# Second layer 7 steps behind instead of 8, Wo's last 64 columns as column-tiled head pairs, FFN up in 128-row chunks plus tails, and a new instruction order

## Chip, cores, metric

One core of one Trainium2 chip. The metric is device time in microseconds (us), the median of several executions. The kernel before takes 2892.89 us (median of 3 runs, 2892.76 to 2893.84).

## The reference

Two identical layers over x of 2048 x 576, bfloat16. Each adds a memory-augmented recurrent attention of the layer norm (32 heads of 128; 64 segments of 32 rows, each with 8 memory rows that the segment before produced), then a gated FFN (576 -> 4608 -> 576) of the layer norm.

```python
for s in range(n_seg):                       # 64 segments, strictly in order
    h = concat([mem, x[:, s*32:(s+1)*32]])   # 40 rows
    q, k, v = h @ Wq, h @ Wk, h @ Wv         # 32 heads x 128
    o = softmax(mask(q @ k.T * scale)) @ v
    o = einsum('bhte,hed->btd', o, Wo)
    mem = o[:, :8]; outs.append(o[:, 8:])
# FFN: (silu(x @ w1) * (x @ w3)) @ w2
```

## The kernel before

Both layers run interleaved: in step t, layer 0 works on segment t and layer 1 on segment t - LAG. So the first and the last LAG steps hold one layer (40 columns, N=40 per matmul) and the steps between two (N=80). FFN groups ("jobs") take 128 rows of one layer or of both (N=128 or 256); jobs 0, 1 and 16 have one layer and run in the first 16 steps and the last ones; job 17 comes after the attention. TensorE's order is a fixed string, one letter for a piece: Q/q are Q,K and their row tail, S scores, T transposes of the probabilities, P times V, O Wo, F/f FFN up and tail, W FFN down, V/v/X/x the values.

```python
LAG = 8
POOLS = {"bank": 7, "y": 1, ..., "ot": 1, ..., "w13": 2, "w2": 3, "htt": 4}
...
def layers_of(t):
    return [li for li in (0, 1) if 0 <= t - LAG * li < nseg]
...
ORDER = FIRST + FOUR * 11 + LAST            # one letter for each piece of TensorE
...
def wo(self, t, g, ot):                     # 8 heads x 5 column blocks
    for hl in range(GH):
        for db in range(5):
            d0 = min(db * P, D - P)         # the last block overlaps the fourth
            self.mm(yT[:, db, :], self.T.WO[:, GH * g + hl, d0:d0 + P], OT[:, hl, :], ...)
...
def ffn_up(self, ents, pr, w13, b, last, tail=None):
    for fb in range(2):
        ...
        for c in ((8,) if tail else range(NCH)):      # NCH = 9 chunks of 64 rows
            for r in (0, 1):                          # gate and up, side by side
                rr = slice(r * R64, (r + 1) * R64)
                self.mm(self.bk(b[r])[:, os_], W[rr, c, fs],
                        self.T.XTB[rr, 4 if tail else POS[c], lo:hi], ..., tile_position=(r * R64, 0))
...
def xtb_write(self, bi, b, split):          # the layer norm, transposed, to both halves
    for r in (0, R64):
        self.cp(n, dst[r:r + R64, 0:4, :], ps[0:R64, 0:4, :])
        self.cp(n, dst[r:r + R64, 4:NCH, :], ps[R64:P, 0:5, :])
```

Of the kernel before, what the change touches and what calls it, by code (L numbers as in the profile page):

```python
# [28 lines left out]
LAG = 8  # L29
# [6 lines left out]

POS = [c // 2 if c % 2 == 0 else 4 + c // 2 for c in range(NCH - 1)] + [8]
POOLS = {"bank": 7, "y": 1, "qkt": 4, "vx": 2, "vm": 1, "sme": 2, "pb0": 1, "pb1": 1, "pts": 1, "ot": 1,
# [10 lines left out]
class Node:  # L49
# [11 lines left out]
    def after(self, *more):  # L61
        for d in more:
# [7 lines left out]
         "WO": "O", "VX": "X", "VXt": "x", "VM": "V", "VMt": "v", "FF": "F", "FFt": "f", "W2": "W"}  # L70
# [108 lines left out]
def ewh(*ns):  # L179
# [5 lines left out]
    "maQQqqXVvxQSQXqQqSTqQPOTqPOSQxqTQqPSOTPXOxQQqqQqSQQqVSqvQTQqqQqPSTOSPOTPTOPaOQQqqQSqXQqQTSxQqqVvSQQqqPSTOPTOPTOP"  # L185
    "OQQqqQQSqVqQSvQqqQTQqPqSXTOSPTOPOTxPXOxQpQqqVSQQqqnvQQSqqFTQQSqPqFOSTFPWTOPFTOPFOXxQQqqQQSqFqQWQSqqFVvSTQQqPqWTO"
    "PSFOTFPTOWPFOaXxQQqqQQqSVqvQSqFQqWTQSPFqQqTOSPTOWPFTOPFOQQqqFVWQqSQvqFQQSqqFTQPqSWQOTqPSFTOPWTOPObVXxvQQqqpQSXqx"
    "QnqQQTSqqQPSFqOQTqFPSFOTPFXxOTWPFOVvQqQQqqFSQQqqXxSQqWTQSPqFOTQqFPSTOWPFXTOxPFOWaQQqqQQSqqQVqSXvxQQqFqWTSQPFTOqP"
    "FSOTFPXWTOxPFOFQQqQqQSqqQqXVvxQqSTSQPqWQOTqPFSOTWPFOTWPObppQXVqxnQqXxQqSQqnQqvQSqQTqFPFSTOQPqWOTSWPFOTXPFFxOWWQQ"
    "qqQSqVXxvQQqqQSqTQSPqFOTQqFPSWTOFPWTOFPFXxWWOQQqqWSVXxvQaTQqqQQSqFqQQSqqFPWTOFPTWOSWPFXTOWPxXOWQqFxQQqFqSQqVQvSQ"  # L190
    "qqQTWqSQWPqFTOPSTOPFOTWPWObVXxvpXxp"
)
FOUR = (
    "QQqqnQnQSqqQQSqqFTQqFPSQTOqPFSOWTWFPFTOXPxWOWQQqqFSQQqqXVxvSWQTQqqFPSQQTOqqFPWTOaSPFXxOTWPFOWQQqqVvSWQQqqFTQQSqq"
    "FPXSxOWTQQqqFFPSWTOWPFOTXxPFWOWQQqqVSvQQqqQQTSqqQQqPqSXxOTFPSWTOWPFTOWPWObVXxvppXx"
)
LAST = (
    "QQqqQSnQqqQQqqSnTQPFqFSTOQPqFSOTWWPFXTOPFOxQQqqXxQQSqqWQSWQqqFFVSvTQqPQqTOPSTOFPXOxTWPWOFQQqqWWQQqqFSSQQqqVXxvWT"
    "QqPSQTqOSFPWTOPFXTOxPWOWQQqFqQQqqFXSxQQSqqFTWQVvqQSqPWOTFPSFOTWWPFOTWPWObVvpQpQqqXxSQQqqnQnSqXxTQQqqQSqFPFTOSPTO"
    "FPFTOPWOWQQqqVWWvSQQqFqQSqQTqQQqqSPFTOXPSxTOWPFOTFPWOFQqQqFSWWQqQQqFqVvSWTWQqFPFTWOQSqPQOWqFTSFPXWFxTOWPFOWQQqqQ"  # L200
    "SQqqVSvQQqqTQSPqQqTOSPWOTFPTOWPOWpbVXvxnQQqqQQSqFqQQSqqXQTxSqQPqFTOSPWTOFPFTOPWOXxFQQqqQSqFVvQTqFSQWQqqFPSQQFqqO"
    "TWPSTOPFOTFPXOFxQWQqqQQSqqQqVSFvQTqQPqFSWQqTOSPFTOPFOTWPOQQqqQQSqVvqFQTqSQqPQSqQqWTSOPOTFPTOPOpnWFfFfFfFWFfFfWfF"
    "fFWfFFWffFfFfWFfFWFffFfWFfFfWW"
# [4 lines left out]
class Opt:  # L208

    qk, qkt, sc, tr, pv, wo, wog, vm = 0.0079, -0.0342, 0.0268, 0.1447, 0.0406, 0.2653, 0.0725, 0.1407  # L210
    vmt, vx, vxt, ff, fft, win, w2, gstep = -0.0231, 0.2313, 0.0843, 0.2124, -0.1839, 3.5294, 0.1943, 0.0624
    ustep, mode_pen, hor, wait, bulk, ff_split, last_win, tail_at = 0.0315, 0.1194, 0.0162, 0.141, 0.02, False, 3.0, -1.5


def make_nodes(em, nseg, pools, o=Opt, dma_bw=230e3, load_bw=340e3):
# [25 lines left out]
    for what, i in [("qk", 0), ("qk", 1), ("v", 0), ("v", 1), ("v", 2), ("v", 3), ("qk", 2), ("qk", 3), ("o", 0),  # L241
                    ("qk", 4), ("qk", 5), ("o", 1), ("qk", 6), ("qk", 7), ("o", 2), ("o", 3)]:
        pr += 0.1
        if what == "qk":
            ld_qk[i] = load("ldqk", kb(1152, 512), pr, em.load_qk(i))
        elif what == "v":
            ld_v[i] = load("ldv", kb(576, 1024), pr, em.load_v(i))
        else:
            ld_o[i] = load("ldo", kb(1024, 576), pr, em.load_o(i))
# [49 lines left out]
    def step(t):  # L299
# [22 lines left out]
        y = Slot("y", users=1)  # L322
        wos = []
        for g in range(NG):
            r, k = g // 2, g % 2
            qs, qe = [], []
            for u in (2 * g, 2 * g + 1):
# [8 lines left out]
                for kind in (0, 1):  # L336
# [22 lines left out]
            wo = node("PE", 40 * mm80, em.wo(t, g, ot), deps=ote + ([ld_o[g]] if t == 0 else []), prio=t + o.wo + o.wog * g, mode="full",  # L359
                      acq=[y] if g == 0 else [], rel=[ot], name="WO")  # L360
            if g:
                wo.after(wos[0])
            wos.append(wo)
            me[f"SC{g}"], me[f"TR{g}"], me[f"PV{g}"], me[f"WO{g}"] = sc, tr, pv, wo
        if t == nst - 1:
            last_reads[1].extend(me[f"QKt{u}"] for u in range(8))
            last_reads[2].extend(wos[:2])
        nxt = [li for li in ls if t - LAG * li + 1 < nseg]
        ye = []
        if nxt:  # L370
            m = 8 * len(nxt)
            ye.append(node("ACT", actc(4 * m), em.y_mem(t, nxt, 0), deps=wos, prio=t - 0.01, name="Ymem"))
            ye.append(node("ACT", actc(m, m), em.y_mem(t, nxt, 1), deps=wos, prio=t - 0.005, name="Ymem"))
            ye[1].after(ye[0])
        ht_mem[t + 1] += ye
        yts = node("ACT", actc(*([160] * nl)), em.yts(t, ls), deps=wos + ye, prio=t + 0.01, rel=[y], name="YTS")
# [3 lines left out]
    def post(li, g):  # L380

        b = banks(1)
        prio = 4 * g + 4 + LAG * li + 0.0
        d = node("PE", 5 * 0.056, em.post_tr(li, g, b[0]), deps=[yx[li, 4 * g + j] for j in range(4)] + ([xr_ld[g]] if li == 0 else []),
                 prio=prio, mode="full", acq=b, name="POST")
        return node("DVE", dve(576), em.post_add(li, g, xr[g], b[0]), deps=[d], prio=prio, rel=b, name="POSTa")
# [4 lines left out]
    def job(j):  # L391
# [6 lines left out]
        s0 = 4 * j + 4  # L398
# [4 lines left out]
        split = last or o.ff_split  # L403
        cost = ewh(512, 128, 128) if split else ewh(512, 640, 512, 640)
        for (bi, g) in ents:
            pa = post(bi, g)
            wr.append(ln_nodes("F", xr[g], Slot("xn"), [pa], s0, (lambda bi=bi: lambda b: em.xtb_write(bi, b, split))(), cost, [prev_ff]))
# [12 lines left out]
        for pp in range(NPR // 2):  # L420
            mids, w2s, htts, lds = [], [], [], []
            for pr_ in (2 * pp, 2 * pp + 1):
# [12 lines left out]
                if split:  # L435
                    fm = node("PE", 16 * mm, em.ffn_up(ents, pr_, w13, b, last, False), deps=wr + ld, prio=prio, mode="full",
                              acq=b + [htt], name="FF")
                    ff = node("PE", 2 * mm, em.ffn_up(ents, pr_, w13, b, last, True), deps=[fm], prio=prio + o.fft, mode="row",
                              rel=rel13, name="FFt")
                else:  # L440
                    ff = node("PE", 18 * mm, em.ffn_up(ents, pr_, w13, b, last), deps=wr + ld, prio=prio, mode="row",
                              acq=b + [htt], rel=rel13, name="FF")
# [12 lines left out]
        for (bi, g) in ents:  # L455
            if bi == 0:
                ht_ready[1, g] = ln_nodes("L1", xr[g], Slot("xn"), w2_last[0], s0 + 3.8,
                                          (lambda g=g: lambda b: em.ht_write(1, g, b))(), HTW, ht_wdeps(4 * g + LAG))
            else:
                xn = Slot("xn")  # L460
                c = node("ACT", actc(576), em.fin_cast(xr[g], xn), deps=w2_last[1], prio=s0 + 3.8, acq=[xn], rel=[xr[g]], name="fin")
                node("SWD", 1.0, em.store(g, xn), deps=[c], prio=s0 + 3.8, rel=[xn], lat=3.0, name="store")
# [17 lines left out]
    for t in range(nst):  # L480
# [7 lines left out]
        if t % 4 == 3:  # L488
            job((t + 1) // 4 - 1)
        if t + 1 < nst:  # L490
# [9 lines left out]
class Emitter:  # L500
# [93 lines left out]
    def load_w13(self, pr, w13):  # L594
        def f(n):
            fa = pr * 2 * P
            for r, wd in ((0, self.a.w1), (R64, self.a.w3)):
                self.dma(self.T.W13[r:r + R64, w13.i], wd[:, fa:fa + 2 * P].rearrange("(c p) f -> p c f", p=R64))
# [113 lines left out]
    def xtb_write(self, bi, b, split):  # L712
        def f(n):
            ps = self.lnps(b)
            dst = self.T.XTB[:, :, bi * P:(bi + 1) * P]
            if split:
                self.cp(n, dst[:, 0:4, :], ps[:, 0:4, :])
            for r in (0, R64):
                if split:
                    self.cp(n, dst[r:r + R64, 4, :], ps[R64:P, 4, :])  # L720
                else:
                    self.cp(n, dst[r:r + R64, 0:4, :], ps[0:R64, 0:4, :])
                    self.cp(n, dst[r:r + R64, 4:NCH, :], ps[R64:P, 0:5, :])
# [187 lines left out]
    def wo(self, t, g, ot):  # L911
        def f(n):
            yT, nq = self.yT(t)
            OT = self.T.OT[:, ot.i, 0:GH * nq].rearrange("p (h q) -> p h q", h=GH)
            for hl in range(GH):
                for db in range(5):
                    d0 = min(db * P, D - P)
                    self.mm(yT[:, db, :], self.T.WO[:, GH * g + hl, d0:d0 + P], OT[:, hl, :],
                            g == 0 and hl == 0 and db == 0, g == NG - 1 and hl == GH - 1 and db == 4)
        return f  # L920

    def y_mem(self, t, nxt, tail):
        def f(n):
# [7 lines left out]
            else:  # L931
                for r in (0, R64):
                    self.cp(n, H_[r:r + R64, 4, c0:c1], v[R64:P, 4])
        return f

    def yts(self, t, ls):
        def f(n):
            yT, _ = self.yT(t)
            j = t % 4
            for li in ls:  # L940
                c0 = XO[li] - ls[0] * QW
                self.cp(n, self.T.YTS[:, li, :, j * SEG:(j + 1) * SEG], yT[:, :, c0:c0 + SEG])
        return f

    def post_tr(self, li, g, b):
        def f(n):
            for db in range(5):
# [15 lines left out]
    def ffn_up(self, ents, pr, w13, b, last, tail=None):  # L963

        def f(n):
            lo, hi = self.span(ents)
            W = self.tail_w[pr][0] if last else self.T.W13[:, w13.i]
            for fb in range(2):
                fs = slice(fb * P, (fb + 1) * P)
                os_ = slice(fb * 2 * P + lo, fb * 2 * P + hi)  # L970
                if tail is False:
                    for r in (0, 1):
                        for c in range(4):
                            self.mm(self.bk(b[r])[:, os_], W[:, 4 * r + c, fs], self.T.XTB[:, c, lo:hi], fb == 0 and c == 0, False)
                    continue
                for c in ((8,) if tail else range(NCH)):
                    for r in (0, 1):
                        rr = slice(r * R64, (r + 1) * R64)
                        self.mm(self.bk(b[r])[:, os_], W[rr, c, fs], self.T.XTB[rr, 4 if tail else POS[c], lo:hi],
                                c == 0, c == NCH - 1, tile_position=(r * R64, 0))  # L980
# [173 lines left out]
```

## Time and profile before

| | value | how to read it |
|---|---|---|
| span | 2885.8 us | the profiled execution, first instruction to last |
| TensorE | 97% busy, x67733 matmuls | busy holds latency too |
| steady four steps | 166 us | eleven alike |
| waits on TensorE, by my sum | 138.8 us | trace minus slots and changes of mode, as in the prediction |

The timeline of TensorE gives start, length, matmuls; in brackets the idle time before.

```profile
2765.05 1.18 PE L519 MATMUL bank<-XTB,W 64*128 64x128 bf16 x36
2766.07 0.36 PE L519 MATMUL bank<-HT,W 64*128 64x40 bf16 x16
2766.36 0.77 PE L519 MATMUL YB<-OT,WO 128*128 128x40 bf16 x24
2769.32 0.57 PE L519 MATMUL YB<-OT,WO 128*128 128x40 bf16 x16 [2.19 <-issue]
```

A single Wo piece of 40 matmuls stops after its 24th for 2.4 us. All its operands were there: the first 24 read the same tiles. No semaphore and no buffer explains a stop in the middle of a piece.

### The profile page before, as it was taken

What the parts mean: (1) busy time and instruction counts of PE and PEld (TensorE: products, weight loads), DVE (VectorE), ACT (ScalarE), POOL (GpSimd) and SP (SyncE); (2) the same over time, 40 slices, a digit from 0 to 9 for tenths busy, and PEclk for the clock granted to TensorE, in tenths of its full rate; (3) what the DMA queues carried; (4) which work ended last, traced back from release to release, by engine and by line L of the source; (5) the groups of instructions that cost most, each with busy time, mean ns of one, the idle gap of its engine ahead of it and who ended that gap; (6) DMA issues with size and microseconds to landing.
All of it is one profiled execution on the core that took longest, in us unless ns stands there. A gap on an engine that the chain in (4) does not pass through costs nothing.

```text
span 2885.8 us, 147090 instructions
## 1 busy us (share of the span) xinstructions
PE 2801.2 (97%) x67733; PEld 2302.7 (80%) x67733; DVE 2077.1 (72%) x5053; ACT 1139.2 (39%) x2933; POOL 63.1 (2%) x110
## 2 busy tenths in 40 slices
PE   5999999999999999999999999999999999999987
PEld 4777878888888878888888888888888888888776
DVE  3667777776777778677777777677777767777765
ACT  1433443343444344344444434344433434343432
POOL 0000000000000000000000000000000000000000
PEclk8999999999999999999999999999999999999999
DMA  9055544434443444444344444534354343436467
GB/s 306 4 130 122 129 98 107 105 90 117 101 106 86 108 107 101 100 109 110 87 107 99 104 101 101 126 88 98 91 120 101 94 118 91 93 97 140 112 159 231
DMA packets 483563, 324.45 MB, mean 112 GB/s; under 512 B 16888, under 2 KB 478080, under 8 KB 482944
## 3 DMA queue, kind: packets, MB, share of 16 engines
q1 hardware_dynamic: 479872, 307.96, 44.3%
q8 instruction: 529, 8.67, 1.3%
q0 software_dynamic: 3072, 7.08, 0.8%
q14 instruction: 90, 0.74, 0.1%
HBM read 310.26 MB, written 2.36 MB: 108 GB/s over the span
## 4 chain that ended last, share of the span: by engine, by line
PE 83%; issue 6%; DVE 5%; DMA 4%; ACT 1%; SPq 1%; POOL 0%; POOLq 0%; DVEq 0%; ACTq 0%
PE bank L519 72%; PE YB L519 10%; DMA W<-in_B_w_dram 2%; DMA W<-in_A_Wk_dram 1%; DVE XR L525 1%; DVE HTT L525 1%; DVE STAT L525 1%; SPq L528 1%; DVE LNS L525 1%; DVE PB L525 1%; DVE SME L525 1%; DMA W2C<-in_B_w_dram 1%; DVE OT L525 0%; DVE XN L525 0%; ACT SME L522 0%
## 5 line engine op out<-in xcount | busy, mean ns | idle before, releaser
L519 PEld LDWEIGHTS <-W 128*128 128x128 bf16 (+1 forms) x34256 | 1231.1, 97 | 124.2 <-issue 34.3
L519 PE MATMUL bank<-HT,W 128*128 128x80 bf16 (+2 forms) x23040 | 805.9, 197 | 13.3 <-ACT HT L522 3.9
L519 PE MATMUL bank<-XTB,W 64*128 64x256 bf16 (+1 forms) x11216 | 616.6, 259 | 6.3 <-DMA W<-in_B_w_dram 4.6
L519 PE MATMUL bank<-WV,HT 128*32 128x512 bf16 (+3 forms) x8000 | 451.6, 384 | 11.3 <-DMA WV<-in_A_Wv_dram 10.1
L519 PE MATMUL YB<-OT,WO 128*128 128x80 bf16 (+1 forms) x11520 | 437.9, 198 | 14.2 <-issue 7.0
L522 ACT ACTIVATE QKT<-bank 128x320 bf16<-128x320 f32 (+1 forms) x773 | 272.9, 409 | 434.1 <-PE bank L519 430.8
L519 PEld LDWEIGHTS <-WO 128*128 128x128 bf16 x11560 | 412.3, 99 | 37.6 <-issue 31.3
L519 PEld LDWEIGHTS <-HT 128*32 128x32 bf16 (+3 forms) x8000 | 172.4, 93 | 219.0 <-issue 68.0
L525 DVE TENSOR_TENSOR PB<-SME,STAT 40x256 bf16<-40x256 f32 (+1 forms) x1024 | 320.5, 318 | 16.6
L519 PE MATMUL bank<-W2C,HTT 128*128 128x288 bf16 x2232 | 324.9, 288 | 5.6 <-DVE HTT L525 2.5
L525 DVE TENSOR_REDUCE STAT<-SME 104x8 f32<-104x320 f32 (+1 forms) x576 | 276.4, 480 | 67.7 <-ACT SME L522 59.9
L522 ACT ACTIVATE HTT<-bank 128x512 bf16<-128x512 f32 (+1 forms) x324 | 177.8, 549 | 341.7 <-PE bank L519 341.6
L525 DVE SCALAR_TENSOR_TENSOR HTT<-HTT,bank 128x512 bf16<-128x512 bf16 (+1 forms) x324 | 201.6, 622 | 107.8 <-ACT HTT L522 103.3
L525 DVE SCALAR_TENSOR_TENSOR XR<-bank,XR 128x288 f32<-128x288 f32 x576 | 245.1, 448 | 32.6 <-PE bank L519 27.8
L525 DVE CAST QKT<-bank 128x320 bf16<-128x320 f32 (+1 forms) x379 | 159.2, 443 | 137.8 <-PE bank L519 135.8
L519 PEld LDWEIGHTS <-HTT 128*128 128x128 bf16 x2304 | 205.0, 98 | 66.7 <-issue 10.5
L522 ACT ACTIVATE PTS<-bank 128x320 bf16<-128x320 f32 (+1 forms) x389 | 146.1, 404 | 197.8 <-PE bank L519 189.9
L525 DVE TENSOR_TENSOR HTT<-HTT,bank 128x512 bf16<-128x512 bf16 (+1 forms) x324 | 203.4, 628 | 23.3 <-DVE HTT L525 1.8
L522 ACT ACTIVATE SME<-SME 104x320 f32<-104x320 f32 (+1 forms) x288 | 135.0, 469 | 192.5 <-DVE SME L525 188.9
L525 DVE TENSOR_TENSOR SME<-bank,maskb 104x320 f32<-104x320 f32 (+1 forms) x288 | 140.1, 487 | 89.1 <-PE bank L519 84.5
L522 ACT ACTIVATE OT<-bank 128x320 bf16<-128x320 f32 (+1 forms) x346 | 133.2, 404 | 162.6 <-PE bank L519 155.9
L522 ACT ACTIVATE VX<-bank 128x512 bf16<-128x512 f32 x166 | 95.1, 596 | 179.7 <-PE bank L519 179.5
(65 smaller groups left out, 1878.4 us busy)
## 6 DMA issues: line engine op xcount, KB each, us to landing
W<-in_B_w_dram SPq DMA_DIRECT2D x612, 288.0 KB, 4.8
W2C<-in_B_w_dram SPq DMA_DIRECT2D x306, 288.0 KB, 3.9
W<-in_B_w_dram SPq DMA_DIRECT2D x10, 512.0 KB, 9.7
XR<-in_A_x_dram POOLq DMA_DIRECT2D x16, 288.0 KB, 3.0
WO<-in_A_Wo_dram SPq DMA_DIRECT2D x4, 1152.0 KB, 8.8
W<-in_A_Wq_dram SPq DMA_DIRECT2D x8, 512.0 KB, 8.5
W<-in_A_Wk_dram SPq DMA_DIRECT2D x8, 512.0 KB, 9.2
WV<-in_A_Wv_dram SPq DMA_DIRECT2D x4, 1024.0 KB, 12.8
```

Of the source, the lines that this page charges most:

```text
L519: self.ch("PE", self.nc.tensor.matmul(out, lhsT=lhsT, rhs=rhs, start=start, stop=stop, skip_group_check=True, **k))
L522: self.ch("ACT", self.nc.scalar.activation(*a, **k))
L525: self.ch("DVE", getattr(self.nc.vector, fn_)(*a, **k))
L528: self.ch("SP", self.nc.sync.dma_start(out=out, in_=in_))
```

## The change

The intent: one step less (lag 7), fewer Wo slots (the fifth block recomputed 64 columns, now two heads share a slot), and FFN chunks that need no change of tile mode and fewer evictions. The order was searched anew. Core of the diff:

```diff
-LAG = 8
+LAG = 7
-... "ot": 1,
+... "ot": 2,
     def wo(...)
-                for db in range(5):
-                    d0 = min(db * P, D - P)
+                for db in range(4):
+    def wo_tail(self, t, g, ot):
+            for hl in range(GH):
+                r = R64 * (hl % 2)
+                self.mm(yT[r:r + R64, 4, :], self.T.WO[:, GH * g + hl, 4 * P:D], OT[:, hl, :], ..., tile_position=(0, r))
+    def y_odd(self, t):                       # ACT copies the odd heads' half, DVE adds it
+            self.cp(n, self.T.YO[:, 0:nq], yT[R64:P, 4, :])
     def ffn_up(...)
-                for c in ((8,) if tail else range(NCH)):   # 18 pairs of 64 rows
+                for r in (0, 1):
+                    if tail:                               # 2 pairs of 64 rows, an own piece
+                        self.mm(..., W[rr, 8, fs], self.T.XTB[rr, 4, lo:hi], ..., tile_position=(r * R64, 0))
+                    else:                                  # 16 matmuls of 128 rows
+                        for c in range(4):
+                            self.mm(..., W[:, 4 * r + c, fs], self.T.XTB[:, c, lo:hi], ...)
     def xtb_write(...)                        # one wide and two small copies for four wide ones
     # FIRST, FOUR, LAST: new strings, with o for a Wo tail; attention weights loaded in another order
-    def store(...): self.swdma(...)
+    def store(...): (self.dma if last else self.swdma)(...)
```

## The prediction

> **What bounds the kernel now.** I read the page first: busy shares, then the slices.
>
> ```profile
> span 2885.8 us, 147090 instructions
> PE 2801.2 (97%) x67733; PEld 2302.7 (80%) x67733; DVE 2077.1 (72%) x5053; ACT 1139.2 (39%) x2933; POOL 63.1 (2%) x110
> ...
> PE   5999999999999999999999999999999999999987
> ...
> PEclk8999999999999999999999999999999999999999
> ```
>
> TensorE is busy everywhere but in the first slice and the last two, at full clock. A matmul's span holds its latency too, so "97%" does not say that it streams all that time. I therefore went to the view by windows, to separate start, steady part and end, and then to the timeline of TensorE, where start-to-start distances give the real price of each piece.
>
> ```profile
> 0.00:70.00 70.00, 38.83 (x844) 27.32 (x846) 26.11 (x70) 12.64 (x34) 6.09 (x18) 0.80 1.06 311
> ...
> 746.00:912.00 166.00, 165.38 (x3862) 136.40 (x3858) 123.55 (x294) 67.78 (x165) 3.80 (x6) 1.00 0.43 102
> ```
>
> Columns: window, length, busy time of PE, PEld, DVE, ACT, POOL, clock, DMA share, GB/s. The first 70 us are bound by the transfer of the attention weights (DMA share over 1, PE 38.8 of 70). A steady period of four steps, 166 us, occurs some eleven times alike; TensorE is busy 165.4 of it, DVE 123.6, DMA 43%.
>
> ```profile
> 763.65 2.13 PE L519 MATMUL bank<-XTB,W 64*128 64x256 bf16 x36
> 765.62 0.20 PE L519 MATMUL bank<-PTS,VX 64*128 64x80 bf16 x2
> ...
> 770.24 2.13 PE L519 MATMUL bank<-XTB,W 64*128 64x256 bf16 x36
> 772.30 0.43 PE L519 MATMUL bank<-QKT 128*64 128x40 bf16 x16
> 772.66 1.61 PE L519 MATMUL YB<-OT,WO 128*128 128x80 bf16 x40
> 774.11 1.15 PE L519 MATMUL bank<-W2C,HTT 128*128 128x288 bf16 x8
> 775.09 0.45 PE L519 MATMUL bank<-sel,PB 104*128 104x80 bf16 x8
> ```
>
> Start to start: the first FFN-up piece lasts 765.62 - 763.65 = 1.97 us for 36 half-row matmuls, that is 18 pairs of 109 ns; its follower is row-tiled as well. The second is followed by a column-tiled piece and lasts 2.06 us: 0.09 more. Wo, 40 matmuls, lasts 1.45 us = 40 x 36 ns, and FFN down 0.98 us = 8 x 122.5 ns, both with no change of tiling after them. Over all neighbouring pieces of the trace, a change of tile mode (full, two row tiles, two column tiles, four column tiles, eight tiles) costs 92 to 103 ns, and no change costs nothing. I use 95 ns.
>
> **What the Trainium skill says.** "TensorE: Matmul & The Clock Gate", section "Back-to-back issue gap", gives N/2.4 + 2.5 ns for a warm matmul of N columns: 35.8 at 80, 109.2 at 256, 122.5 at 288. The trace agrees (36, 109, 122.5). The same page, table "Why this matters for your kernels", says that K=32 takes the same time as K=128 and that the gain is concurrency. The trace agrees for K=64: the pair costs one slot of 109 ns. "TensorEngine Tiling (Array Packing)", section "Key Properties", says that changing the tiling mode drains the engine: 95 ns here. Its "Restrictions" say that column tiling disables fast weight load. The column-tiled scores show what is left: 16 matmuls of N=40, with 64 columns loaded in one column group, take 0.36 us with the switch, so about 33 ns a pair. That is below the 36 ns that a pair at N=80 streams anyway.
>
> **The change part by part.** I write TensorE's time as slots (matmuls by slot, a pair counting once) plus 95 ns for each change of mode, counted along both programs' own instruction order. For the kernel before: 2569.7 us of slots and 1759 changes (167.1 us), 2736.8 us. From TensorE's first matmul to its last the trace has 2875.6 us, so 138.6 us are waits and cold clock: 39 in step 0, 40 in steps 1 to 15, 37 from step 60 on, and some 23 spread over the 44 steps between. In the steady period slots and changes give 155.5 + 90 x 0.095 = 164.1 of the 166.0 us.
>
> *Lag 7 for 8.* Two steps with one layer go, and one with two layers comes: 72 steps become 71. Old prices: one-layer step 17.6 us of slots (QK with tails 7.2, Wo 4.0, V 3.9, scores, transposes and PV 2.5), two-layer step 25.2 (10.3, 5.7, 5.8, 3.3). Saved: 2 x 17.6 - 25.2 = 9.9 us.
>
> *Wo's last 64 columns in pairs.* Per head group 40 slots become 32 + 4 column pairs: 4 slots less. 57 two-layer steps x 4 groups x 4 x 35.8 ns = 32.7 us, 14 one-layer steps x 4 x 4 x 25 ns = 5.6 us (25 ns is what a matmul of N=40 takes in the trace). Saved: 38.3 us of slots. But the piece is column-tiled: unless it stands beside scores or another tail, it needs a switch in and out, 190 ns, against a saving of 143 ns.
>
> *FFN up in 128-row chunks.* 36 half-row matmuls (18 pair slots) become 16 full ones and 2 pairs: 18 slots. Saved: nothing, though there are 16 x 306 = 4896 fewer matmuls and weight loads. The big part now shares its mode with QK, Wo and FFN down; the small row tail must find a row-tiled neighbour. The four wide evictions per layer norm (ACT 699 and 587 ns each) become one of 597 and two of 272 ns: that relieves ACT and DVE, which do not bind.
>
> *Changes of mode.* Counted in the new order: 2217, 458 more, 43.5 us. Without the Wo tails it would be 1986, so 231 are theirs and 227 come with the split FFN and the order. In the steady period 90 become 114, while slots fall from 155.5 to 153.2: 164.1 us again. The two effects cancel there almost exactly.
>
> *Sum on TensorE:* -9.9 - 38.3 + 43.5 = -4.7 us; 2.1 us of it lie in step 0, which waits for weights anyway: -2.6. About 5 ns that each piece costs beyond the formula, by 556 more pieces: +2.8.
>
> *Waits.* For each link of the chain (scores to probability transpose, that to PV, PV to Wo, Wo to the next step's QK, FFN up to down) I took the shortest latency that stalled pieces show in the trace (4.1, 0.7, 0.77, 0.47 us, about 2.6) and the slots that stand between the two in each order. Where the slots fall short, TensorE waits. These shortfalls after step 0 sum to 30.7 us before and 17.5 after: 0.97 to 0.18 us a period in the steady part (-8.7 in all), -2.8 before it, -1.7 at the end. So -13.2 us. The start's remaining waits (weights, banks, colder clock) and the end's I leave unchanged. The last store goes to a hardware queue: about -0.8, an estimate from the 0.58 us that GpSimd spends on issuing such a store.
>
> Total: -2.6 + 2.8 - 13.2 - 0.8 = -13.8 us, 2892.9 -> **2879 us**.
>
> **The rivals.** (1) *The Wo saving arrives whole*, because switches hide behind streaming: 43 us less, about 2836. Against it: in the trace every switch shows up start to start, whatever the neighbours. (2) *Column tiles load slowly*: if the two halves' loads took turns, a pair would take some 70 ns instead of 36, 284 x 4 x 35 ns = +40 us, 2919. Against it: scores, tiled in the same way, run their two columns of work side by side. (3) *The memory chain becomes the wait.* Wo's tail now needs a copy of the odd half on ACT (about 0.23, from the 219 ns of a 64-column copy), a hop, and two additions on DVE, before the row tail of the next QK: about 0.95 us with 0.27 us of drain and hand-over, an estimate from PV to Wo. The slots between are at least 1.24 us in the middle, 3.0 in the median, 1.7 at the least in the one-layer steps. It fits, but DVE runs in order at 74% and an operation of 0.69 us may stand ahead. Half a us lost in each step would be +35 us, 2914. (4) *The FFN is pressed into three steps* and waits for weights or DVE. Each weight set takes five issues instead of three, at about 0.6 us: 52 us of SyncE in 164; DMA stands at 43%. Only bursts could wait: +5 to +15. (5) *The order removes more waits than links show* (banks, engine queues, cold clock in the start): another -10 to -20, about 2865.
>
> **Range and chances.** The TensorE sum is good to some 10 us (a switch 5 ns dearer or cheaper moves the difference by only 2 us, a Wo tail 30 ns dearer by 9), the waits to 15. Eight in ten: 2858 to 2899. Two per cent is 58 us; 2835 needs rival 1 and 2951 needs rival 3 on every step. Faster by over 2%: 0.04; within: 0.94; slower: 0.02.
>
> **What would show it.** 62221 matmuls; a steady period of 164.5 to 166 us; a Wo tail of about 0.14 us start to start plus 0.09 for each change; full FFN chunks 109 ns apart; TensorE's first 70 us as before; few waits after the copy of the odd half. A steady period of 162 or less would prove rival 1, of 168 or more rivals 2 to 4. If the gain lies in the first 300 us rather than in the steady part, my split of the waits was wrong.

## More of the kernel before

All runs quoted here are undisturbed.

The prediction shows the page's head, the windows and a steady timeline. One view it passed over is the waits of TensorE, whole run, sorted by sum (engine, tile, what it waited for: us in total, times, longest):

```profile
PE bank L519 <- issue: 13.7, 18, 2.2
...
PE YB L519 <- issue: 7.0, 8, 2.4
```

"issue" means that the profile shows nothing that TensorE waited for. These 20.7 us were the largest named wait of the kernel. They lie at its two ends.

## The result, and the profile after

The changed kernel takes **2851.28 us** (median of 4, 2849.08 to 2855.76) against 2892.82 (median of 4) beside it: ratio 0.9861, 95% interval 0.9844 to 0.9878, so 41.5 us by the medians where 14 were predicted, and below the predicted range. (A ratio here is the mean time of one kernel's fast runs over that of the other's of the same rounds, so not quite the ratio of the medians quoted.)

The page's lines that answer to those of before (part 3's columns are packets, MB, share), then the windows of both kernels. The windows' columns are those that the prediction names:

```profile
span 2847.9 us, 137052 instructions
PE 2784.7 (98%) x62221; PEld 2269.2 (80%) x62221; DVE 2129.7 (75%) x5300; ACT 1076.2 (38%) x2808; POOL 58.8 (2%) x110
...
PEclk9999999999999999999999999999999999999998
```

Before:

```profile
70.00:100.00 30.00, 27.61 (x876) 23.53 (x875) 18.54 (x56) 12.50 (x41) 0.00 (x0) 0.89 0.06 15
200.00:270.00 70.00, 64.21 (x1856) 51.42 (x1852) 43.56 (x122) 23.11 (x78) 1.62 (x3) 0.95 0.48 114
```

After:

```profile
70.00:100.00 30.00, 29.67 (x928) 22.96 (x925) 20.05 (x58) 12.03 (x43) 0.00 (x0) 1.00 0.02 4
200.00:270.00 70.00, 68.45 (x1780) 55.36 (x1779) 50.83 (x140) 30.07 (x88) 1.89 (x3) 1.00 0.33 93
746.00:912.00 166.00, 165.68 (x3575) 135.48 (x3571) 128.30 (x314) 63.70 (x159) 3.14 (x7) 1.00 0.36 103
```

The steady window looks the same in both (165.4 and 165.7 us busy of 166). The early windows do not: from 200 to 270 us TensorE was busy 64.2 of 70 us at clock 0.95, and is now busy 68.5 at full clock. In the same time DVE did 122 instructions before and 140 after.

To place the gain I cut both traces at the same steps, counted slots and changes of mode along each program's order as in the prediction, and call "waits" what is left (cold clock included):

| steps | before: us / sum of slots and changes / waits | after | change of the waits |
|---|---|---|---|
| 1 to 11 | 338.1 / 303.5 / 34.6 | 335.0 / 320.1 / 14.9 | -19.7 |
| 12 to 15 | 177.5 / 172.1 / 5.4 | 170.9 / 168.0 / 2.8 | -2.6 |
| 16 to 59 | 1827.7 / 1804.9 / 22.8 | 1828.3 / 1804.7 / 23.5 | +0.7 |
| 60 to 66 | 276.4 / 270.1 / 6.3 | 286.1 / 278.4 / 7.6 | +1.3 |
| 67 on | 190.8 / 160.3 / 30.5 | 154.9 / 136.9 / 18.1 | -12.4 |

The sums shrink by 2.6 us over these rows before rounding, as predicted (they are the same count along the orders, so they test no price). Step 0 with its lead-in went from 68.3 to 67.2 us, and the end after the last matmul's start shrank by 1.55 us. With 32.7 us of waits this makes the 37.9 us by which the two spans differ. Single traces scatter: three later kernels with the changed kernel's order have 17.5 to 17.9 us of waits in steps 1 to 11 and 19.6 to 20.1 from step 67 on, so about 5 of these 32.7 us are luck of the profiled run.

The waits views say the same. Steps 1 to 15 of the before kernel (64 to 400 us), first three lines:

```profile
PE bank L519 <- issue: 5.5, 9, 1.7
PE bank L519 <- DMA W<-in_B_w_dram: 3.4, 5, 1.2
PE YB L519 <- issue: 1.9, 4, 0.7
```

and of the kernel after:

```profile
PE bank L521 <- ACT HT L524: 2.3, 6, 0.7
PE YB L521 <- ACT OT L524: 0.8, 2, 0.4
```

At the end (2640 us on), before and then after:

```profile
PE bank L519 <- issue: 8.2, 9, 2.2
PE YB L519 <- issue: 4.6, 2, 2.4
```

```profile
PE bank L521 <- issue: 3.5, 2, 3.3
```

What went is the kind "issue", 12.8 us of it at the end of which 3.5 stay; at the start 7.4 us, of which next to nothing stays.

**A cause for "issue".** Part 3 of the page has a row of packets for TensorE's instructions, before and then after:

```profile
q8 instruction: 529, 8.67, 1.3%
```

```profile
q8 instruction: 486, 7.96, 1.1%
```

A packet is 8.67 MB / 529 = 16 KiB. A matmul is two instructions (weight load and multiply), and 2 x 67733 / 529 = 256; after, 2 x 62221 / 486 = 256. So TensorE's instructions come in pages of 256. I numbered TensorE's instructions and looked at where in its page each wait stands:

| before: next piece starts at | us lost | inside | after matmul | place in the page of 256 |
|---|---|---|---|---|
| 202.3 | 1.55 | Q tail | 7 of 8 | 186 |
| 228.8 | 0.69 | Q | 31 of 32 | 186 |
| 243.6 | 1.84 | transposes | 3 of 8 | 186 |
| 258.4 | 0.80 | Wo | 23 of 40 | 186 |
| 2749.1 | 0.56 | Q tail | 8 of 8 | 174 |
| 2764.2 | 0.87 | Q | 12 of 32 | 174 |
| 2769.7 | 2.38 | Wo | 24 of 40 | 174 |
| 2831.3 | 2.55 | Wo | 8 of 40 | 174 |

Different pieces, different matmuls, the same place. From 2740 to 2836 us there are 12 waits of over 0.5 us, and 10 of them stand at 174. The Trainium skill, "Runtime: NRT & Kernel Launch", section "Instruction fetch mechanics", says that instructions are refilled in 16 KiB blocks of 256, fetched over the sequencer's own DMA queue while the current block runs; the packets above agree. It also calls the cost of crossing a block "mostly hidden". In this trace it is not. The fetches of two pages never start closer than 3.3 us, rarely under 3.7. That is 256 / 3.7 = 69 instructions per us, 78 at the very best. Where TensorE starved, the supply was lower still: from 2741 to 2767 us fetches started 4.4 to 5.7 us apart, 45 to 58 instructions per us.

The DMA packets of the trace, each with its start, tie the waits to the fetches: all 26 waits called "issue" of over 0.3 us after step 0 stand at places 174 to 186 and end 2.4 to 3.0 us after a fetch began, while the 54 other waits of that size end anywhere from 0.0 to 7.6 us after one. What the pieces ask for:

| piece | instructions per us |
|---|---|
| matmul of N=40 (one layer) | 2 in 25 ns: 80 |
| FFN up, one layer, row pair of N=128 | 4 in 55.8 ns: 72 |
| FFN up, one layer, 128-row chunk | 2 in 55.8 ns: 36 |
| matmul of N=80 (two layers) | 2 in 35.8 ns: 56 |
| FFN up, two layers, row pair of N=256 | 4 in 109 ns: 37 |

With one layer, Q, K, Wo and the kernel before's FFN up ask for instructions as fast as or faster than they come; FFN down, 2 in 122.5 ns, does not. The chunks halve the demand of FFN up, and the fetch can catch up there. With two layers the demand is lower: 332 fetches in the 1827.7 us of steps 16 to 59, 46 instructions per us. This theory says where the gain must lie (one-layer stretches) and which part of the change makes it (the chunks). The experiments test it.

### The profile page after: what moved, and what is told of

The parts are those of the page before. It is cut to its first block, busy times and chain, and to the rows that moved or that the text cites. A ratio compares the mean times of both kernels' runs of the same rounds, so it can differ in the third digit from the quotient of the medians.

```text
span 2847.9 us, 137052 instructions
## 1 busy us (share of the span) xinstructions
PE 2784.7 (98%) x62221; PEld 2269.2 (80%) x62221; DVE 2129.7 (75%) x5300; ACT 1076.2 (38%) x2808; POOL 58.8 (2%) x110
## 4 chain that ended last, share of the span: by engine, by line
PE 92%; issue 4%; DMA 1%; DVE 1%; ACT 1%; SPq 0%; POOL 0%; DVEq 0%; ACTq 0%; POOLq 0%
PE bank L521 80%; PE YB L521 13%; DMA W<-in_A_Wk_dram 1%; DMA WV<-in_A_Wv_dram 0%; DVE HTT L527 0%; ACT HT L524 0%; DVE STAT L527 0%; DMA W2C<-in_B_w_dram 0%; DVE SME L527 0%; SPq L530 0%; DVE XR L527 0%; DVE QKT L527 0%; DVE PB L527 0%; ACT PTS L524 0%; DVE OT L527 0%
## 5 line engine op out<-in xcount | busy, mean ns | idle before, releaser
L521 PEld LDWEIGHTS <-W 128*128 128x128 bf16 (+1 forms) x29040 | 1212.5, 98 | 142.3 <-issue 56.4
L521 PE MATMUL bank<-HT,W 128*128 128x80 bf16 (+3 forms) x22720 | 821.5, 197 | 10.2 <-issue 5.7
L521 PE MATMUL bank<-XTB,W 128*128 128x256 bf16 (+3 forms) x6320 | 659.5, 262 | 0.1
L524 ACT ACTIVATE QKT<-bank 128x320 bf16<-128x320 f32 (+1 forms) x714 | 262.2, 409 | 487.0 <-PE bank L521 459.4
L521 PE MATMUL YB<-OT,WO 128*128 128x80 bf16 (+3 forms) x11360 | 434.8, 199 | 7.1 <-ACT HT L524 4.4
L521 PEld LDWEIGHTS <-WO 128*128 128x128 bf16 (+1 forms) x11400 | 389.7, 102 | 58.2 <-issue 43.7
L527 DVE TENSOR_TENSOR PB<-SME,STAT 40x256 bf16<-40x256 f32 (+1 forms) x1024 | 321.4, 318 | 16.7
L521 PE MATMUL bank<-W2C,HTT 128*128 128x288 bf16 x2232 | 315.5, 287 | 1.8 <-DVE HTT L527 1.0
L527 DVE CAST QKT<-bank 128x320 bf16<-128x320 f32 (+1 forms) x422 | 183.8, 455 | 169.9 <-PE bank L521 167.4
L524 ACT ACTIVATE HTT<-bank 128x512 bf16<-128x512 f32 (+1 forms) x324 | 177.5, 549 | 237.6 <-PE bank L521 236.9
L524 ACT ACTIVATE OT<-bank 128x320 bf16<-128x320 f32 (+1 forms) x364 | 140.5, 406 | 185.1 <-PE bank L521 183.3
L527 DVE TENSOR_TENSOR SME<-bank,maskb 104x320 f32<-104x320 f32 (+1 forms) x284 | 137.4, 488 | 61.8 <-PE bank L521 57.9
L527 DVE CAST OT<-bank 128x320 bf16<-128x320 f32 (+1 forms) x204 | 94.3, 463 | 80.2 <-PE bank L521 77.3
```

The lines of the kernel that those rows point to most:

```text
L521: self.ch("PE", self.nc.tensor.matmul(out, lhsT=lhsT, rhs=rhs, start=start, stop=stop, skip_group_check=True, **k))
L524: self.ch("ACT", self.nc.scalar.activation(*a, **k))
L527: self.ch("DVE", getattr(self.nc.vector, fn_)(*a, **k))
```

## The experiments

All were timed in three rounds beside the kernel before (median 2886.97 in the first four, 2892.96 in the next four, 2894.37 and 2894.35 in the last two calls). "Page waits" below are waits of over 120 ns at places 170 to 192 of a page, counted after step 0 from each trace. Before has 31.4 us of them, after 5.5. This count goes by place alone: it takes in 3.5 us before 2846.4 us, at place 176, which the trace puts down to the last layer norm (DVE XN), and some shorter waits on data. Counting only those called "issue", before has 26.0 us, after 4.5, run 1 4.8, run 3 16.7 and run 4 28.4.

**1. Chunks in the one-layer FFN groups alone, added to the kernel before.**

```diff
-        split = last or o.ff_split
+        split = last or j in (0, 1, 16)      # each F of these groups followed by its tail f; copies and W loads in chunk form
```

> The kernel before, with 128-row FFN chunks and tails in the three one-layer FFN groups alone (the fourth has them already). TensorE's sum of slots and mode changes rises from 2736.8 to 2744.8 us (84 changes more); 864 matmuls and weight loads fewer, all in the one-layer part. Theory 1, TensorE starves for its own instructions where narrow matmuls use up a 256-instruction page in under some 4 us: waits in steps 1 to 11 and from 67 on fall by 12 to 20 us, time 2881 to 2889. Theory 2, the waits were ones on data, banks and order: they stay, time 2901.

Measured: 2867.06 us (2866.16 to 2867.76), ratio 0.9932 [0.9916, 0.9949]: 19.9 us faster, more than the 4 to 12 that theory 1 expected, although its sum of slots and changes is 8.0 us higher (84 more changes). About 28 us of waits are gone, 15.4 of them in steps 1 to 11 and 12.4 from step 67 on. Page waits fell from 31.4 to 7.4 us. The same stretch of the end now runs, in its timeline:

```profile
2764.88 1.27 PE L534 MATMUL bank<-XTB,W 128*128 128x128 bf16 x20
...
2767.24 1.14 PE L534 MATMUL bank<-W2C,HTT 128*128 128x288 bf16 x8
2768.21 2.96 PE L534 MATMUL bank<-HT,W 128*128 128x40 bf16 x112
2771.10 0.37 PE L534 MATMUL bank<-QKT 128*40 128x40 bf16 x8
```

The 112 matmuls (96 full ones of N=40, and 16 half-row ones of two Q tails, which run in pairs), nearly a page by themselves, run through in 2.89 us without a stop, behind two pieces that ask for little.

A rival stays untested: the edit also changes how these groups load W and copy XTB, so the fetches could have gained from lighter DMA traffic. Against it: a fetch's packet took 1.13 us in steps 1 to 11 before and 1.07 in this run; and from step 67 on the DMA engines were 56% busy both before and after the whole change.

**2. Chunks in all groups, in the order of before.**

```diff
+        split = last or j in (0, 1, ..., 16)
```

> The kernel before, with the FFN chunks everywhere and its old order (each tail right behind its chunk piece). Slots unchanged, 519 more mode changes: sum 2786.1, +49 us. Theory 1: minus 12 to 20 at the start and end, time 2922 to 2930. Theory 2: 2942. A rival to both, the chunks stream faster than pairs: under 2915.

Measured: 2908.97 us (2908.77 to 2910.18), ratio 1.0078 [1.0063, 1.0094]. Steps 16 to 59 went from 1827.7 to 1863.9 us with 352 more changes of mode, 33.4 us by the 95 ns of the prediction; their waits hardly moved (22.8 to 25.6). With two layers a chunk saves no time on instructions and costs its switches: it needs an order that seats the tails. The total is 22.0 us above the kernel before of its round, where theory 1 expected 29 to 37 and the rival of faster chunks some 22 or less. The rival does not follow all the same: the steady steps got no cheaper than priced; steps 1 to 11 and those from 67 on lost some 29 us of waits, more than theory 1's 12 to 20.

**3. Half-row pairs back in the one-layer groups of the changed kernel.**

```diff
+FF_ROWS = (0, 1, 16)
-        cost = ewh(512, 128, 128)
+        split = last or j not in FF_ROWS     # and ffn_up, copies and weight load of before for these
```

> The changed kernel with the three one-layer FFN groups back to half-row pairs. Sum of slots and changes 2731.8 against 2732.1, so no difference there; 864 matmuls more. Theory 1: waits come back at the start and the end, +12 to +20 us, 2863 to 2871. Theory 2: 2851, no difference.

Measured: 2872.94 us (2871.65 to 2876.16), ratio 0.9954 [0.994, 0.9969]. That is 21.7 us above the changed kernel by medians, 27 by the two ratios. Waits in steps 1 to 11 rose from 14.9 to 29.8 us, from step 67 on from 18.1 to 28.3; page waits from 5.5 to 19.7. The steady part did not move (1828.3 and 1828.2). Theory 1 expected 12 to 20. So the one-layer chunks (with their copies and loads) are worth 20 to 27 us from either side: half of the whole gain or more.

**4. The kernel before with 80 TensorE instructions more at its start.**

```diff
+            for _ in range(40):              # 40 small matmuls of no use
+                self.mm(self.T.YB[:, 400:408], self.T.ident[:], self.T.ident[:, 0:8], True, True)
```

> The kernel before with 40 small matmuls (80 instructions) put ahead, in the time in which the first weights load; nothing else. Time as before, within 3 us. Theory 1: the waits of over 0.3 us that stood at place 174 to 186 of a 256-instruction page stand at the same places again, 80 instructions earlier in the kernel's own order, so before other matmuls than in the kernel before. Theory 2: they stand before the same matmuls, so at a place that is 80 further on in the page.

Measured: 2894.56 us (2893.01 to 2897.55), ratio 1.0029 [1.0014, 1.0044]. That is 7.6 us slower than the kernel before of its round, where at most 3 were expected; by the cut traces, steps 1 to 11, 60 to 66 and those from 67 on take about 3 us more each. If the waits belonged to points of the program, they would now stand 80 places further, at 254 and at 10. They stand at 174 and 188 again, behind other matmuls:

| with 80 instructions ahead: next piece starts at | us lost | inside | after matmul | place |
|---|---|---|---|---|
| 252.7 | 1.88 | FFN up | 28 of 36 | 188 |
| 2743.8 | 1.14 | P times V | 16 of 16 | 174 |
| 2750.4 | 1.72 | Wo | 20 of 40 | 174 |
| 2780.3 | 2.07 | Wo | 24 of 40 | 174 |
| 2837.0 | 1.95 | Q | 32 of 32 | 174 |

This separates the page from every wait of the program's own. That the fetch is what TensorE waits for is inferred from this, from the page length and from the packets: here too the 24 "issue" waits of over 0.3 us end 2.2 to 3.0 us after a fetch began. No record names the fetch as the releaser.

**5. The changed kernel with Wo in five full blocks again.**

```diff
-ORDER = FIRST + FOUR * 11 + LAST
+ORDER = (FIRST + FOUR * 11 + LAST).replace("o", "")   # and wo, y_mem, yts as before
```

> The changed kernel with Wo as five full column blocks again (the tails taken out of the order). Slots +38.3 us, 231 mode changes fewer: sum 2748.5 against 2732.1, so +16 us: 2867. If the tails' saving were eaten wholly by their switches: 2851 or less. If the tails streamed free of switches: 2851 + 38 = 2889.

Measured: 2869.99 us (2866.94 to 2870.61), ratio 0.9919 [0.9904, 0.9934]; 16.8 us above the changed kernel by the ratios, where its sum is 16.4 higher. Each of the two ratios is good to some 5 us. The traces are closer: steps 16 to 59 take 11.9 us more, where the sum is 13.2 higher. In this order the Wo pairs are worth about their slots minus their switches.

**6. Lag and order alone: Wo as before, FFN in row pairs in every group (two W2 buffers, for memory).**

```diff
+FF_ROWS = (0, 1, ..., 16)
+ORDER = _rows(ORDER).replace("o", "")        # and wo, ffn_up as before
```

> Lag 7, new order and new order of weight loads alone: neither Wo tails nor FFN chunks (and one W2 buffer less, for room). Sum 2759.6 against 2732.1 of the changed kernel: +27.5. Theory 1 (instruction starvation was cured by the chunks): the waits at start and end come back as well, 2890 to 2898. Theory 2 (lag and order cured the waits): 2879.

Measured: 2955.86 us (2952.93 to 2956.84), ratio 1.0219 [1.0202, 1.0236]. My expectation was far off. Page waits returned at both ends (6.7 us to step 15, 10.5 from step 67), but 38 us more of waits also stood in the steady part (61.8 against 23.5), which no theory here had. Run 9 takes this up.

**7. The changed kernel with two W2 buffers** (a control for 6, 8 and 9).

```diff
-         "w13": 2, "w2": 3,
+         "w13": 2, "w2": 2,
```

> The changed kernel with two W2 buffers instead of three: the control for the runs that need the room. No difference, 2851, within 3 us.

Measured: 2855.93 us (2852.97 to 2858.38), ratio 0.9872 [0.9857, 0.9887]: 3.2 us above the changed kernel by the ratios, whose intervals overlap; a difference is not shown.

**8. All four Wo tails of a step together.**

```diff
-         ... "ot": 2, ... "w2": 3
+         ... "ot": 4, ... "w2": 2
+            if c == "o": n += 1; c = "oooo" if n % 4 == 0 else ""
```

> The changed kernel with the four Wo tails of a step together behind the last Wo (four output buffers, two W2 buffers). 127 mode changes fewer, 12.1 us: 2839. If each change were partly hidden, less than 8. If the later release of buffers adds waits: 2851 or more.

Measured: 2857.88 us (2857.46 to 2859.19), ratio 0.988 [0.9865, 0.9895]. It has 127 fewer changes of mode, 12.1 us, and is no faster than run 7: against it, steps 16 to 59 shrank by 4.5 us (66 of the changes, 6.3 us), while waits in steps 1 to 11 rose from 17.9 to 25.9 and from step 67 on from 20.1 to 22.5. That the late tails are what is waited for is likely, not shown.

**9. The changed kernel with row pairs in all groups, Wo tails kept** (for run 6).

```diff
+FF_ROWS = (0, 1, ..., 16)
-         "w13": 2, "w2": 3,
+         "w13": 2, "w2": 2,
```

> The changed kernel (same order, Wo tails kept) with FFN up as 18 pairs of half-row matmuls in every group, two W2 buffers. Slots and changes of mode along its own order: 2743.5 us against 2732.1 (+11.4). One-layer groups as in a_rows_narrow, which came out some 17 us above two-buffer versions of the changed kernel; of its waits about 14 us lay at fixed places in the instruction page. Theory A (the 38 us of unexpected waits in the steady part of a_lag_only come from wide row pairs run in an order that was searched for chunks: longer evictions ahead of them, both banks needed at once): the steady part, steps 16 to 59, is 35 to 60 us over the changed kernel's 1828, total 2905 to 2930. Theory B (they come from what a_lag_only undid besides, Wo's full width in that order): the steady part is at most 15 us over, total 2875 to 2888.

Measured: 2948.21 us (2942.82 to 2950.87), ratio 1.0185 [1.0168, 1.0202]. Steps 16 to 59 take 1884.5 us, 55.5 above run 7: 11.5 are 121 more changes of mode, 44 are waits. That is theory A's range for the steady part; the total is above it, because waits came back in steps 1 to 15 and at the end too. (The "17 us" of its expectation set run 3, which has three buffers, against run 7 with two; against the changed kernel it is the 21.7 of run 3.) The waits of TensorE from 600 to 2450 us, this kernel:

```profile
PE bank L542 <- ACT QKT L545: 13.6, 22, 0.6
PE bank L542 <- ACT XTB L545: 9.7, 22, 0.5
PE YB L542 <- ACT HT L545: 3.5, 11, 0.3
```

and run 7:

```profile
PE YB L521 <- ACT HT L524: 3.5, 11, 0.3
```

The timeline of TensorE and that of ACT show one of the places:

```profile
954.31 0.27 PE L542 MATMUL bank<-XTB,W 64*128 64x256 bf16 x1
955.03 0.29 PE L542 MATMUL bank<-XTB,W 64*128 64x256 bf16 x2 [0.45 <-ACT XTB L545]
955.75 2.01 PE L542 MATMUL bank<-XTB,W 64*128 64x256 bf16 x33 [0.44 <-ACT XTB L545]
```

```profile
953.08 2.62 ACT L545 ACTIVATE XTB<-bank 64x512 bf16<-64x512 bf16 x4
```

The wide copies are on the path. In this kernel ACT makes 120 of the 124 wide copies, in the kernel before 64, with DVE making the other 60: the new order, searched for one wide copy and two small ones, leaves them to ACT, and FFN up starts too soon behind them. Whether another order would hide them again, as before's does, was not tried. So 6 is explained in kind: form and order belong together.

**10. Tails moved next to column-tiled neighbours.**

```diff
-ORDER = FIRST + FOUR * 11 + LAST
+ORDER = (...)                                # 37 letters "o" moved, 2178 changes of mode for 2217
```

> The changed kernel with 37 of its Wo tails moved beside a column-tiled neighbour in the instruction order: 2178 changes of mode instead of 2217, -3.7 us of TensorE's sum, nothing else altered. If the sum sets the time: 2847.5 against 2851.3. Rival (as a_gather showed: every moved tail shifts the waits elsewhere): within 1 us of the changed kernel, or slower.

Measured: 2852.43 us (2850.27 to 2855.43), ratio 0.9857 [0.9842, 0.9872]: the same as the changed kernel. A gain of 3.7 us is neither shown nor excluded.

**11. Attention weights in the load order of before.**

```diff
-    ... ("qk", 2), ("qk", 3), ("v", 0), ("v", 1), ("v", 2), ("v", 3), ("qk", 4), ...
+    ... ("v", 0), ("v", 1), ("v", 2), ("v", 3), ("qk", 2), ("qk", 3), ("o", 0), ...
```

> The changed kernel with the attention weights loaded in the order of the kernel before (V's before the second half of Q/K's). If the start is bound by the total transfer, the first 70 us and the time stay within 3 us of the changed kernel (2849 to 2855). If the new load order is what lets step 0 and the first steps go without cold clock: 5 to 12 us slower, and TensorE's clock in the first steps falls again.

Measured: 2854.29 us (2852.06 to 2856.41), ratio 0.9861 [0.9844, 0.9878]: within 3 us. The gain at the start is not the load order's.

**12. The last store by GpSimd, as before.**

```diff
-        (self.dma if last else self.swdma)(...)
+        self.swdma(...)
```

> The changed kernel with its last store issued by GpSimd again, as in the kernel before. If the queue was worth the 0.8 us that I predicted, 2852 against 2851.3, and from the last matmul's start to the end of the span about 5.2 us instead of 4.4; if all of the shortening at the end that the traces show (5.94 to 4.39 us) is the store's, 5.9 us and 2852.8. Rival: the end is set by something else, and neither moves (4.4 us, 2851.3).

Measured: 2854.72 us (2850.95 to 2857.39), ratio 0.9859 [0.9842, 0.9876], too coarse for this question, but the trace answers it: from the last matmul's start to the end 5.95 us, against 4.39 with the hardware queue and 5.94 in the kernel before. The queue is worth 1.55 us.

None of the variants is shown to beat the changed kernel.

## Why the prediction was wrong

**TensorE's sum: right but for the price of a Wo tail.** The traces check its prices: 62221 matmuls came, a two-layer chunk took 109.3 ns, a change about 95. A two-layer Wo tail of four pairs took 0.165 us with no change behind it and 0.266 with one (medians), so 41 ns a pair where 35.8 were priced: some 5 us in all, far from the 40 of rival 2. So the reading of the scores, 33 ns a pair at N=40 and hence no loss at N=80, did not carry over. (A slip: 2875.6 - 2736.8 is 138.8, not 138.6.) In the timeline after:

```profile
756.66 1.91 PE L521 MATMUL bank<-XTB,W 128*128 128x256 bf16 x16
758.41 0.45 PE L521 MATMUL bank<-sel,PB 104*128 104x80 bf16 x8
...
760.69 0.33 PE L521 MATMUL YB<-OT,WO 128*64 128x80 bf16 x8
760.86 0.41 PE L521 MATMUL bank<-QKT 128*64 128x40 bf16 x16
```

16 chunks last 758.41 - 756.66 = 1.75 us with no change behind them; the tail 760.86 - 760.69 = 0.17, its neighbour being column-tiled too. In steps 16 to 59, run 2's changes of mode cost 36.2 us where 33.4 were priced; run 5 gave 16.8 for 16.4. Rivals 1 and 2 fall.

**The failed step: "The start's remaining waits (weights, banks, colder clock) and the end's I leave unchanged."** I had sized the waits well (40 us in steps 1 to 15, 37 from step 60) and split off 4.5 us of link shortfalls, before the steady part and at the end. The rest I named from habit. In steps 1 to 11 they fell by 17 to 20 us, from step 67 on by 10 to 12. The largest kind was neither weights nor banks but instructions, some 26 us of page waits, and the line "issue: 13.7" lay in the view of waits. The cold clock moved with them: half clock for 17.1 us in steps 1 to 11 before, for 6.8 with the one-layer chunks alone (run 1), for none after (0 to 7.6 in three later kernels with its order), and with row pairs back in the one-layer groups (run 3) for 11.9. That it is a consequence is not shown.

Behind it stands the line "FFN up in 128-row chunks ... Saved: nothing, though there are 16 x 306 = 4896 fewer matmuls and weight loads." I priced a matmul by its stream and gave its delivery no price. In one-layer groups that delivery was the limit, and runs 1 and 3 put the chunks at 20 to 27 us.

**Steady waits: -8.7 us predicted, +0.7 measured.** The links that I counted did shrink: stalls of over 150 ns in steps 16 to 59 fell from 9.4 to 5.6 us. But one new wait of 0.51 us per period came, before the last Wo tail: ACT copies part of YB to HT while the last tail is to write the same bank.

```profile
1035.30 1.57 PE L521 MATMUL YB<-OT,WO 128*128 128x80 bf16 x40
1037.19 0.33 PE L521 MATMUL YB<-OT,WO 128*64 128x80 bf16 x8 [0.32 <-ACT HT L524]
```

```profile
1036.91 0.23 ACT L524 ACTIVATE HT<-YB 128x64 bf16<-128x64 f32 x1 [2.07 <-PE YB L521]
```

And what pieces cost beyond the formula rose from 13.4 to 18.0 us. The 5 ns a piece of the prediction was the wrong term: the 176 Wo tails took 23 ns each, 4.1 us of the rise, the 198 FFN tails 6 ns. The steady period was 166.2 us in both kernels (the 44 steps of the table by 11): neither the 162 of rival 1 nor the 168 of rivals 2 to 4. My test named this case: "If the gain lies in the first 300 us rather than in the steady part, my split of the waits was wrong." It was, at the end too.

**Rival 5 was right in kind**, "more waits than links show", and held the cold clock, but named the order. The order is not the cause of this part: run 1 kept the old one.

**The store: -0.8 predicted, -1.55 measured,** as run 12 shows. Its issuing took 0.54 us on GpSimd and 0.37 on SyncE, which explains 0.17; the rest lies after the issue and has no record.

**Open:** why a starved TensorE stops at place 174 or 186 of its page and not at its end; what holds fetches 3.3 us apart and more, when a packet itself takes 1.3% x 16 x 2885.8 / 529 = 1.1 us; how much of the cold clock's cost is the instructions'; and what the other half of the gain beyond the sum owes to lag and order, because run 6, meant to isolate them, made new waits of its own.

## What to carry to other kernels

Count instructions per us for each stretch beside its streaming time: small-N matmuls, and row pairs above all, can ask for them faster than they are delivered, and then one matmul over 128 rows beats two side by side over 64 at equal slots. A wait called "issue" that stops a piece in its middle deserves its place in the page of 256 before any other explanation. An order that was searched for one form of a piece is not a neutral place to try another form.

## What the Trainium skill lacked or had wrong

- "Runtime: NRT & Kernel Launch", section "Instruction fetch mechanics", calls the fetch of instructions mostly hidden, because instructions are dispatched more slowly than they come in. Here it cost some 26 us of waits at fixed places of the page, up to 2.6 us each; page fetches never started less than 3.3 us apart, rarely under 3.7, so 69 to 78 instructions per us at best (45 to 58 where TensorE starved), while N=40 matmuls with their loads ask for 80.
- "TensorE: Matmul & The Clock Gate", section "Back-to-back issue gap", gives a sustained spacing of about 81 ns for a stream of loads and matmuls of N=128. Here 16 chunks of N=128, each with its own weight load, took 0.99 us with one change of mode behind them, so (0.99 - 0.095) / 16 = 55.9 ns each, as the section's formula for an isolated matmul, which the prediction used, gives (55.8).
- "TensorEngine Tiling (Array Packing)" says that a change of tile mode drains the engine, without a price: 95 ns here, in the steady part and in runs 2 and 5. It has no price for a column pair of 64 columns each either: 41 ns at N=80.
- "DMA: Bandwidth & Descriptors" tells the two queues apart, but not by what a last store costs in all: from the last matmul's start to the end of the span, 5.95 us by GpSimd and 4.39 by the hardware queue, for the same work.
